# Decoding 64-bit weights on the chip: two scaled ScalarE copies and two VectorE passes in place of five VectorE passes, given out one step after the load

## The chip, the core and the metric

The kernel runs on one core of one Trainium2 chip. The core has five engines with a queue each: TensorE (PE in the profile; its weight loads are PEld), VectorE (DVE), ScalarE (ACT), GpSimd (POOL) and SyncE (SP), which here issues every DMA. An engine takes its own instructions in the order in which the program gives them out; between engines it is semaphores that order the work. The metric is the device time of one execution in microseconds, the median of the runs shown; lower is better.

## The reference

Three stages follow one another: an attention with decay over 2 batches of 8 heads, 768 tokens and 64 channels, and then two gated layers over the resulting 1536 x 512 activations.

```python
# per block of 64 tokens, with Dmask[i, j] = lam ** (i - j) for i >= j, else 0
out   = (q @ k.T * Dmask) @ v + (q * lam ** (pos + 1)) @ kv_state
kv_state = lam ** 64 * kv_state + (k * lam ** (63 - pos)).T @ v
# then, x being 1536 x 512
h = x @ w_in;   x = (h * tanh(softplus(h))) @ w_out      # layer 1, mish
h = x @ w_in2;  x = (h * sigmoid(h)) @ w_out2            # layer 2, silu
```

The four weight matrices are 512 x 2048 or 2048 x 512 and arrive as 64-bit floating-point numbers; q, k, v and lam are 32-bit.

## The kernel before

**Tiles.** The tokens are 12 chunks of 128 for the attention (n = 0 to 11, six to a batch) and three blocks of 512 for the layers (t = 0, 1, 2). The inner dimension of a layer, 2048, is cut into 16 tiles of 128; counted through both layers they are n = 0 to 31. A weight half (n, i) is one of them: (n, 0) is the 128 x 512 tile of w_in, (n, 1) that of w_out. There are 64 halves. Each is decoded once, to 32 bits, and then split in two: `wh` is the value rounded to TensorE's 32-bit matmul type by ScalarE, `wl` is what is left, by a subtraction on GpSimd (`run_parts`, L173). The activations are split in the same way (`xh`, `xl`; `gh`, `gl`), and every product is three matmuls: high by high, low by high, high by low.

**How a half comes in.** `load_w` (L71) takes one of four `slot` buffers and has SyncE issue its DMA of 512 KB. A 64-bit number lies in the slot as a low and a high 32-bit word next to each other, so a pass over the high words reads every second word. `split_w` (L86) registers a half; `begin` gives it one of four `dec` buffers; five VectorE passes (`split_op`, L122) decode it: L130 clears the sign of the high word, L132 clamps it from below, L134 shifts and masks, L136 puts in three bits of the low word, L138 puts back the sign. For the last 25 halves L94 does the first of them on ScalarE (`Abs`). After the fifth pass the slot goes back to the list, which lets `pump` (L610) load the next half. For ten pairs of tiles four more VectorE subtractions (`sum_pair`, L145, L164) make sums `t` of weights, which are split into `th`, `tl`.

**What sets the order.** The order of every engine is that in which this code calls it; nothing reorders. The code goes by steps. In each, `run_split(k)` gives out the next k VectorE passes of the list `todo`, `run_parts` the splits of the halves that are decoded, and then the step's matmuls are called. The k of each step are hand-written numbers (L634, L665, L681, L728 to L732). A VectorE or ScalarE instruction therefore stands behind all that was called before it on its engine, whether it needs that or not.

**The stages.** In the first four steps (L620) only attention chunks are worked on; x arrives in 1 MB loads that share SyncE's queue with the weights. In steps i = 0 to 7 (L643) a chunk of attention, a `w_in` product of layer 1 (`emit_h`, PE L418, then `wa` by ScalarE L399, `gh` L402, `gl` by GpSimd L403) and a `w_out` product (`emit_o`, PE L443) alternate. Within a chunk: `emit_S` (PE L305) makes scores, VectorE masks them into `sm` (L307), `emit_kd` and `emit_qd` scale k and q (ScalarE L289, GpSimd L282 and L294), GpSimd decays the state (L313), PE L326 makes `pc`, VectorE adds it to the state (L336), PE L344 and L350 make `px`, and ScalarE copies `px` to `xf` and `xh` (L358, L359). `emit_S` of the next chunk takes the two buffers that `pc` and `px` leave, so from the seventh chunk on it waits for L358.

Then come eight groups g of four tiles, less the first, which the steps above did. In the groups that begin a layer all products are plain. In the others a pair of tiles is a `Block` (L536), a fast 2 x 2 scheme whose seven products m1 to m7 (PE L557, six matmuls each) stand in the order m1, m5, m2, m6, m7, m3, m4. After m1 ScalarE copies bank `a` to bank `b` (L576), and m2 goes on accumulating in `a`, so m2 waits for that copy. In a group's second block, B, m1, m5 and m2 follow one another with nothing between; in its first block, A, a `w_out` product stands between m5 and m2. Just ahead of B, the last product of t = 2 of the group before ends and VectorE adds it to `acc` (L467, `evac`).

## Time and profile before

| | |
|---|---|
| time, median of 3 runs | 588.62 us (588.27 to 588.92) |
| span of the profiled execution | 584.0 us |
| TensorE busy | 565.3 us, 97% of the span |
| VectorE busy | 409.0 us, 70% |
| GpSimd busy | 317.1 us, 54% |
| ScalarE busy | 235.6 us, 40% |
| mean granted TensorE clock | 0.997 of full speed |

The span runs from the first to the last instruction of the profiled execution. That execution's own time is the span and what lies around it (start and end of the program), and the page gives the span alone; the median of the runs is 4.6 us above it. In a row of the timeline the columns are the start in us from the span's start, the duration in us, the engine, the line, the operation, what it writes and reads, how many instructions are merged in the row, and in brackets the idle time ahead of it with what ended that.

### The profile page before, as it was taken

What the parts mean: (1) busy time and instruction counts of PE and PEld (TensorE: products, weight loads), DVE (VectorE), ACT (ScalarE), POOL (GpSimd) and SP (SyncE); (2) the same over time, 40 slices, a digit from 0 to 9 for tenths busy, and PEclk for the clock granted to TensorE, in tenths of its full rate; (3) what the DMA queues carried; (4) which work ended last, traced back from release to release, by engine and by line L of the source; (5) the groups of instructions that cost most, each with busy time, mean ns of one, the idle gap of its engine ahead of it and who ended that gap; (6) DMA issues with size and microseconds to landing.
All of it is one profiled execution on the core that took longest, in us unless ns stands there. A gap on an engine that the chain in (4) does not pass through costs nothing.

```text
span 584.0 us, 7516 instructions
## 1 busy us (share of the span) xinstructions
PE 565.3 (97%) x2882; PEld 461.5 (79%) x2882; DVE 409.0 (70%) x509; ACT 235.6 (40%) x431; POOL 317.1 (54%) x233
## 2 busy tenths in 40 slices
PE   7689989999999999999999999999999999999997
PEld 5577768888878888888888877887888888888885
DVE  3897872769999687857798898649743993486112
ACT  2434343255424333334345465457333643344120
POOL 1767675335556364726578476737633764454320
PEclk8999999999999999999999999999999999999999
DMA  7954730003312222212312122312201140200103
GB/s 255 424 204 145 288 101 10 1 0 109 108 38 78 68 72 73 74 37 70 110 40 68 36 72 75 105 38 82 99 28 59 59 143 2 72 1 1 73 8 136
DMA packets 14627, 50.55 MB, mean 87 GB/s; under 512 B 1528, under 2 KB 3072, under 8 KB 13312
## 3 DMA queue, kind: packets, MB, share of 16 engines
q1 hardware_dynamic: 14592, 50.08, 25.1%
q8 instruction: 22, 0.36, 0.2%
q14 instruction: 13, 0.11, 0.1%
HBM read 46.92 MB, written 3.15 MB: 86 GB/s over the span
## 4 chain that ended last, share of the span: by engine, by line
PE 80%; DVE 12%; ACT 2%; DMA 2%; issue 1%; POOL 1%; SPq 0%; ACTq 0%; POOLq 0%
PE po L443 40%; PE ph L418 21%; PE b L557 7%; PE a L557 4%; PE c L557 2%; DVE dec L136 2%; PE e L557 2%; DVE dec L138 2%; DVE dec L134 1%; PE s L305 1%; DVE dec L132 1%; DVE sm L307 1%; DMA lamrow<-scr 1%; PE px L344 1%; PE px L350 1%
## 5 line engine op out<-in xcount | busy, mean ns | idle before, releaser
L403 POOL TENSOR_TENSOR gl<-wa,gh 128x512 fp32r<-128x512 f32 x96 | 144.0, 1505 | 115.1 <-PE b L557 40.4
L179 POOL TENSOR_TENSOR wl<-dec,wh 128x512 fp32r<-128x512 f32 x64 | 88.9, 1389 | 95.9 <-ACT wh L178 93.9
L467 DVE TENSOR_TENSOR acc<-po,acc 128x512 f32<-128x512 f32 x72 | 46.4, 686 | 67.0 <-PE po L443 66.9
L399 ACT ACTIVATE wa<-ph 128x512 f32<-128x512 f32 x56 | 33.6, 599 | 139.0 <-PE ph L418 135.1
L418 PE MATMUL ph<-xh,wh 128*128 128x512 f32 x224 | 87.5, 391 | 0.2 <-ACT xh L359 0.2
L418 PE MATMUL ph<-xl,wh 128*128 128x512 f32 x224 | 85.7, 389 | 0.0
L443 PE MATMUL po<-gh,wh 128*128 128x512 f32 x192 | 75.9, 395 | 0.0
L443 PE MATMUL po<-gh,wl 128*128 128x512 f32 x192 | 74.9, 390 | 0.8 <-POOL wl L179 0.8
L443 PE MATMUL po<-wh,gh 128*128 128x512 f32 x192 | 74.8, 390 | 0.5 <-ACT acc L465 0.5
L443 PE MATMUL po<-wl,gh 128*128 128x512 f32 x192 | 74.9, 390 | 0.3 <-POOL wl L179 0.3
L443 PE MATMUL po<-wh,gl 128*128 128x512 f32 x192 | 74.7, 389 | 0.0
L132 DVE TENSOR_SCALAR dec<-dec 128x512 f32<-128x512 f32 x64 | 45.4, 709 | 34.2 <-ACT dec L94 33.1
L138 DVE SCALAR_TENSOR_TENSOR dec<-slot,dec 128x512 uint32<-128x512 uint32 x64 | 67.9, 1061 | 1.9
L136 DVE SCALAR_TENSOR_TENSOR dec<-slot,dec 128x512 uint32<-128x512 uint32 x64 | 63.6, 994 | 2.1
L178 ACT CAST wh<-dec 128x512 fp32r<-128x512 f32 x64 | 39.6, 619 | 60.1 <-DVE dec L138 60.1
L418 PE MATMUL ph<-xh,wl 128*128 128x512 f32 x224 | 61.4, 389 | 0.0
L402 ACT CAST gh<-wa 128x512 fp32r<-128x512 f32 x96 | 58.7, 623 | 1.1
L134 DVE TENSOR_SCALAR dec<-dec 128x512 uint32<-128x512 uint32 x64 | 51.3, 802 | 2.0
L443 PE MATMUL po<-gl,wh 128*128 128x512 f32 x192 | 52.0, 393 | 0.0
L418 PEld LDWEIGHTS ph<-xh,wh 128*128 128x128 f32 x224 | 42.0, 188 | 9.4 <-ACT xh L359 0.4
L418 PEld LDWEIGHTS ph<-xh,wl 128*128 128x128 f32 x224 | 42.0, 188 | 8.8
L418 PEld LDWEIGHTS ph<-xl,wh 128*128 128x128 f32 x224 | 42.0, 188 | 8.8
(107 smaller groups left out, 874.7 us busy)
## 6 DMA issues: line engine op xcount, KB each, us to landing
slot<-w SPq DMA_DIRECT2D x64, 512.0 KB, 3.7
xslot<-x SPq DMA_DIRECT2D x10, 1024.0 KB, 9.4
out<-acc SPq DMA_DIRECT2D x12, 256.0 KB, 2.0
xslot<-x SPq DMA_DIRECT2D x4, 512.0 KB, 4.3
dmask<-scr SPq DMA_DIRECT2D x2, 256.0 KB, 4.0
lamrow<-scr SPq DMA_DIRECT2D x2, 128.0 KB, 6.0
pw<-lam SPq DMA_DIRECT2D x1, 0.0 KB
scr<-pw SPq DMA_DIRECT2D x1, 8.0 KB
```

Source lines behind the costliest of these rows:

```text
L132: nc.vector.tensor_scalar(out=df, in0=df, scalar1=2.0**-15, scalar2=None, op0=ALU.max)
L134: nc.vector.tensor_scalar(out=d, in0=d, scalar1=3, scalar2=0x3FFFFFF8, op0=shl, op1=band)
L136: nc.vector.scalar_tensor_tensor(out=d, in0=low, scalar=29, in1=d, op0=shr, op1=bor)
L138: nc.vector.scalar_tensor_tensor(out=d, in0=high, scalar=0xC0000000, in1=d, op0=band, op1=bor)
L178: nc.scalar.copy(hi, f)
L179: nc.gpsimd.tensor_tensor(out=lo, in0=f, in1=hi.bitcast(F32), op=ALU.subtract)
L402: nc.scalar.copy(gh, a)
L403: nc.gpsimd.tensor_tensor(out=gl, in0=a, in1=gh.bitcast(F32), op=ALU.subtract)
L418: nc.tensor.matmul(ph, lhsT=wi[wsel][:, kk * P : (kk + 1) * P], rhs=xt[xsel][:, kk, :], start=(i == 0), stop=(i == 3 * KD - 1),)
L443: nc.tensor.matmul(po[t][j], lhsT=lhsT, rhs=rhs, start=(first and wsel + gsel == 0), stop=(last and gsel == 1))
L467: nc.vector.tensor_tensor(out=acc[:, j, :], in0=po[t][j], in1=acc[:, j, :], op=ALU.add)
L557: nc.tensor.matmul(self.b[dst], lhsT=w[ws][:, kk * P : (kk + 1) * P], rhs=x[xx][:, kk, :], start=(start and i == 0), stop=(i == 5), skip_g ...
```

## The change

The five passes become four, on two engines. ScalarE copies the high words, read as 32-bit floats and scaled by 2^-112, to `dec`; it then copies the low words, read as integers, in place in the slot, scaled and shifted so that the three bits remain that L136 took by a shift. VectorE shifts `dec` left by three and puts in the three bits (new L126), and puts back the sign (new L130). All 64 halves go this way; the `Abs` copies are gone.

The order changes too. A counter `tick` goes up at the end of each step. `begin`, which now holds the two ScalarE copies, runs for a half at the earliest in a later step than its load was issued in (`age`), and the VectorE passes at the earliest in a later step than `begin`. The hand-written k are gone: `run_split(2)` is called in nearly all steps, `run_split(1)` in a `Block`'s, and `run_pre` starts one half, or two in an attention step. In the attention the halves are registered all ten at once, so that they no longer wait for the step that named them. In the groups `run_parts` is called ahead of the step's matmuls for all that is decoded. The matmuls stand in the same order as before.

```diff
     def load_w(n, i):
+        loaded[n, i] = tick[0]
@@
-            if on_act:
-                nc.scalar.activation(decs[n, i].bitcast(F32), raws[n, i][:, :, 1].bitcast(F32), AF.Abs)
+            begun[n, i] = tick[0]
+            low, high = raws[n, i][:, :, 0], raws[n, i][:, :, 1]
+            nc.scalar.activation(decs[n, i].bitcast(F32), high.bitcast(F32), AF.Copy, scale=2.0**-112)
+            nc.scalar.activation(low, low, AF.Copy, scale=TOP3, bias=2.0**-21 - 0.5)
@@
-            if k == 4:
+            if k == 1:
                 slots.append(held.pop((n, i)))
                 parts.append((*wtiles[n, i], decs[n, i].bitcast(F32), (n, i)))
@@
-    def run_pre(now=False):
-        while pre and (now or (len(uses) < WD and pre[0][0] in raws)):
-            assert len(uses) < WD
+    def run_pre(k=1, age=1):
+        while k and pre and len(uses) < WD and pre[0][0] in raws and tick[0] - loaded[pre[0][0]] >= age:
             pre.pop(0)[1]()
-            now = False
+            k -= 1
@@
         if k == 0:
-            nc.vector.tensor_scalar(out=d, in0=high, scalar1=0x7FFFFFFF, scalar2=None, op0=band)
-        elif k == 1:
-            nc.vector.tensor_scalar(out=df, in0=df, scalar1=2.0**-15, scalar2=None, op0=ALU.max)
-        elif k == 2:
-            nc.vector.tensor_scalar(out=d, in0=d, scalar1=3, scalar2=0x3FFFFFF8, op0=shl, op1=band)
-        elif k == 3:
-            nc.vector.scalar_tensor_tensor(out=d, in0=low, scalar=29, in1=d, op0=shr, op1=bor)
+            nc.vector.scalar_tensor_tensor(
+                out=d, in0=d, scalar=3, in1=low, op0=ALU.logical_shift_left, op1=ALU.bitwise_or
+            )
         else:
-            nc.vector.scalar_tensor_tensor(out=d, in0=high, scalar=0xC0000000, in1=d, op0=band, op1=bor)
+            nc.vector.scalar_tensor_tensor(
+                out=d, in0=high, scalar=0x80000000, in1=d, op0=ALU.bitwise_and, op1=ALU.bitwise_or
+            )
@@
     def run_split(k):
-        for _ in range(min(k, len(todo))):
-            todo.pop(0)()
-        run_pre()
+        while k and todo and (todo[0][0] is None or begun.get(todo[0][0], tick[0]) < tick[0]):
+            todo.pop(0)[1]()
+            k -= 1
@@ attention, first four steps
         if n == 1:
-            split_w(0, 0)
-        if n == PH - 2:
-            split_w(1, 0)
-            split_w(0, 1)
-        run_split((0, 3, 5, 3)[n])
+            for half in ((0, 0), (1, 0), (0, 1), (2, 0), (1, 1), (3, 0), (2, 1), (3, 1), (4, 0), (5, 0)):
+                split_w(*half)
+        run_split(2)
         finish = emit_O(n)
+        run_pre(1 + (n == PH - 1))
@@ steps i
-        run_split((6, 3, 4, 4, 4, 4, 4, 4, 4, 0, 0, 0)[i])
+        run_split(2)
...
             xfinish = emit_O(n)
+        run_pre(2)
...
-        run_split((2, 0, 4, 4, 4, 4, 4, 4, 0, 0, 0, 5)[i])
+        run_split(2)
         pump()
+        tick[0] += 1
@@ groups
             run_later()
-            k = len(parts)
+            run_parts()
+            if item[0] is idle or item[0] in fills or item[0] in os:
+                run_pre()
             for fn in item:
                 fn()
-            run_parts(k)
...
-            run_split(k)
+            run_split(1 if isinstance(getattr(item[0], "__self__", None), Block) else 2)
             pump()
+            tick[0] += 1
```

VectorE in the third step of the attention, from the state of chunk 1 to the mask of chunk 3; `sm<-s` are the masks, two to a chunk, and slot_84 holds the first half. Before:

```order
L336 TENSOR_TENSOR state_101<-pc,state_101 64x4x64 x2
L130 TENSOR_SCALAR dec<-slot_84 128x512
L132 TENSOR_SCALAR dec<-dec 128x512
L134 TENSOR_SCALAR dec<-dec 128x512
L307 TENSOR_TENSOR sm<-s_265,dmask 128x512
L307 TENSOR_TENSOR sm<-s_266,dmask 128x512
```

After:

```order
L330 TENSOR_TENSOR state_101<-pc,state_101 64x4x64 x2
L301 TENSOR_TENSOR sm<-s_264,dmask 128x512
L301 TENSOR_TENSOR sm<-s_265,dmask 128x512
L356 TENSOR_TENSOR xl<-xf,xh 128x4x128
L330 TENSOR_TENSOR state_102<-pc,state_102 64x4x64 x2
L126 SCALAR_TENSOR_TENSOR dec<-dec,slot_84 128x512
L130 SCALAR_TENSOR_TENSOR dec<-slot_84,dec 128x512
```

The three passes that stood between the state of chunk 1 and the mask of chunk 2 are gone, and the two that are left stand behind that mask.

ScalarE in step i = 1, from the `xh` of chunk 5 to the `xf` of chunk 6. Before:

```order
L359 CAST xh<-xf 128x4x128
L402 CAST gh<-wa 128x512
L399 ACTIVATE wa<-ph 128x512
L178 CAST wh_480<-dec 128x512
L289 ACTIVATE kd<-xslot_109,dmask 128x64 x4
L358 COPY xf<-px 128x512
```

After:

```order
L353 CAST xh<-xf 128x4x128
L98 ACTIVATE dec<-slot_86 128x512
L99 ACTIVATE slot_86<-slot_86 128x512
L98 ACTIVATE dec<-slot_87 128x512
L99 ACTIVATE slot_87<-slot_87 128x512
L396 CAST gh<-wa 128x512
L172 CAST wh_460<-dec 128x512
L393 ACTIVATE wa<-ph 128x512
L172 CAST wh_533<-dec 128x512
L283 ACTIVATE kd<-xslot_109,dmask 128x64 x4
L352 COPY xf<-px 128x512
```

Four copies and one more rounding to `wh` now stand between two `xf` copies.

ScalarE at the start of block B of the third group (g = 2): the copy of bank `a` to bank `b`, and what stands ahead of it. `th` is the upper half of a sum of weights. Before:

```order
L399 ACTIVATE wa<-b 128x512
L402 CAST gh<-wa 128x512
L178 CAST wh_1811<-dec 128x512
L576 COPY b<-a 128x512
L581 COPY m_1924<-e 128x512
```

After:

```order
L393 ACTIVATE wa<-b 128x512
L396 CAST gh<-wa 128x512
L98 ACTIVATE dec<-slot_86 128x512
L99 ACTIVATE slot_86<-slot_86 128x512
L172 CAST th<-t_1826 128x512
L570 COPY b<-a 128x512
L172 CAST wh_1807<-dec 128x512
L575 COPY m_1891<-e 128x512
```

VectorE at the same place, after the change:

```order
L158 TENSOR_TENSOR t_1826<-dec 128x256
L158 TENSOR_TENSOR t_1826<-dec,t_1826 128x256
L158 TENSOR_TENSOR t_1826<-dec 128x256
L461 TENSOR_TENSOR acc<-po,acc 128x512 x4
L158 TENSOR_TENSOR t_1826<-dec,t_1826 128x256
L126 SCALAR_TENSOR_TENSOR dec<-dec,slot_85 128x512
L130 SCALAR_TENSOR_TENSOR dec<-slot_85,dec 128x512
```

The `th` that now stands ahead of the copy needs the fourth subtraction, and that now stands behind the four additions to `acc`; before, the subtractions of this pair were all ahead of them.

## Rows read from the trace of the kernel before

**Rows 1.** Engines' busy time, share of the span and instructions, from the page.

```profile
PE 565.3 (97%) x2882; PEld 461.5 (79%) x2882; DVE 409.0 (70%) x509; ACT 235.6 (40%) x431; POOL 317.1 (54%) x233
```

**Rows 2.** Busy time by stretch: length, then PE, PEld, DVE, ACT, POOL, clock, DMA.

```profile
17.87:99.19 81.32, 72.34 (x643) 57.02 (x642) 64.08 (x90) 34.10 (x76) 56.22 (x47) 1.00 0.52 193
99.19:340.00 240.81, 240.81 (x1077) 198.72 (x1076) 194.25 (x223) 96.15 (x163) 132.41 (x90) 1.00 0.19 61
340.00:410.00 70.00, 68.72 (x300) 55.62 (x299) 54.35 (x56) 38.68 (x70) 47.06 (x32) 1.00 0.24 76
410.00:578.35 168.35, 168.35 (x744) 139.41 (x743) 86.74 (x121) 60.94 (x108) 76.04 (x56) 1.00 0.15 51
```

**Rows 3.** Timeline of PE, 17 to 100 us: where it waits, and three scores.

```profile
21.75 0.43 PE L350 MATMUL px<-sm,xslot 128*64 128x128 f32 x2 [1.01 <-DVE sm L307]
...
28.64 0.43 PE L350 MATMUL px<-sm,xslot 128*64 128x128 f32 x2 [2.42 <-DVE sm L307]
...
42.78 1.16 PE L344 MATMUL px<-qd,state 128*128 128x128 f32 x8 [1.34 <-POOL qd L294]
...
53.23 1.16 PE L305 MATMUL s<-xslot 64*128 64x128 f32 x14 [0.29 <-ACT xf L358]
...
64.51 1.16 PE L305 MATMUL s<-xslot 64*128 64x128 f32 x16 [0.25 <-issue]
...
74.25 1.52 PE L305 MATMUL s<-xslot 64*128 64x128 f32 x16
...
87.14 1.16 PE L305 MATMUL s<-xslot 64*128 64x128 f32 x14 [0.81 <-ACT xf L358]
...
96.91 1.16 PE L305 MATMUL s<-xslot 64*128 64x128 f32 x16
```

**Rows 4.** Timeline of DVE ahead of the first wait of rows 3.

```profile
18.15 1.17 DVE L130 TENSOR_SCALAR dec<-slot 128x512 uint32<-128x512 uint32 x1
```

**Rows 5.** Timelines of ACT and POOL in the attention.

```profile
21.96 1.07 ACT L289 ACTIVATE kd<-xslot,dmask 128x64 f32<-128x64 f32 x4 [2.74 <-DMA xslot<-x]
...
85.03 0.62 ACT L178 CAST wh<-dec 128x512 fp32r<-128x512 f32 x1 [2.64 <-DVE dec L138]
...
26.31 1.27 POOL L179 TENSOR_TENSOR wl<-dec,wh 128x512 fp32r<-128x512 f32 x1 [2.01 <-ACT wh L178]
```

**Rows 6.** Groups by line: count, busy us and mean ns, idle before.

```profile
L134 DVE TENSOR_SCALAR dec<-dec 128x512 uint32<-128x512 uint32 x64 | 51.3, 802 | 2.0
...
L132 DVE TENSOR_SCALAR dec<-dec 128x512 f32<-128x512 f32 x64 | 45.4, 709 | 34.2 <-ACT dec L94 33.1
...
L130 DVE TENSOR_SCALAR dec<-slot 128x512 uint32<-128x512 uint32 x39 | 30.6, 785 | 0.0
...
L94 ACT ACTIVATE dec<-slot 128x512 f32<-128x512 f32 x25 | 16.0, 671 | 1.1 <-DMA slot<-w 0.8 <-POOL wl L179 0.3
...
L358 ACT COPY xf<-px 128x512 f32<-128x512 f32 x12 | 6.9, 576 | 7.3 <-PE px L350 7.3
...
L450 ACT CAST sh<-tmp 128x1024 fp32r<-128x1024 f32 x2 | 2.1, 1062 | 0.0
```

**Rows 7.** Timelines of DVE, PE and ACT at the start of block B, group 2.

```profile
208.69 2.48 DVE L467 TENSOR_TENSOR acc<-po,acc 128x512 f32<-128x512 f32 x4 [2.13 <-PE po L443]
...
210.53 0.62 PE L557 MATMUL e<-sh,th 128*128 128x512 f32 x2
...
210.72 0.57 ACT L576 COPY b<-a 128x512 f32<-128x512 f32 x1 [1.21 <-PE a L557]
...
211.88 0.62 PE L557 MATMUL a<-xh,wh 128*128 128x512 f32 x2
```

**Rows 8.** Timeline of DVE: the shortest and the longest weight subtraction here.

```profile
199.42 0.42 DVE L164 TENSOR_TENSOR t<-dec,t 128x256 f32<-128x256 f32 x1
...
364.66 1.52 DVE L164 TENSOR_TENSOR t<-dec 128x256 f32<-128x256 f32 x1
```

**Rows 9.** DMA issues of weight halves: count, KB each, us to landing, from the page.

```profile
slot<-w SPq DMA_DIRECT2D x64, 512.0 KB, 3.7
```

More of the change, by code (lines that the diff above doesn't have):

```diff
@@ L74, in load_w @@
         raws[n, i] = held[n, i].bitcast(U32).rearrange("p (c two) -> p c two", two=2)
+    TOP3 = 2.0**-29 * (1 - 2.0**-20)
+    tick = [0]
+    loaded, begun = {}, {}
     ready = set()
@@ L106, in split_w @@
         pre.append(((n, i), begin))
-        todo.extend(lambda k=k: op(k) for k in range(int(on_act), 5))
-    def run_pre(now=False):
-        while pre and (now or (len(uses) < WD and pre[0][0] in raws)):
-            assert len(uses) < WD
+        todo.extend(((n, i), lambda k=k: op(k)) for k in range(2))
+    def run_pre(k=1, age=1):
+        while k and pre and len(uses) < WD and pre[0][0] in raws and tick[0] - loaded[pre[0][0]] >= age:
             pre.pop(0)[1]()
-            now = False
+            k -= 1
     def used(key):
@@ L169, in op @@
                 used((b, 0))
-        todo.extend(lambda k=k: op(k) for k in range(4))
+        todo.extend((None, lambda k=k: op(k)) for k in range(4))
     def run_parts(k=None):
@@ L629, in decay_attention_mish_silu_kernel @@
         if n == 1:
-            split_w(0, 0)
-        if n == PH - 2:
-            split_w(1, 0)
-            split_w(0, 1)
-        run_split((0, 3, 5, 3)[n])
+            for half in ((0, 0), (1, 0), (0, 1), (2, 0), (1, 1), (3, 0), (2, 1), (3, 1), (4, 0), (5, 0)):
+                split_w(*half)
+        run_split(2)
         finish = emit_O(n)
+        run_pre(1 + (n == PH - 1))
         run_parts()
         pump()
+        tick[0] += 1
     later.append(finish)
-    halves = {0: [(2, 0)], 1: [(3, 0), (1, 1)], 3: [(2, 1), (3, 1), (4, 0), (5, 0)]}
     for i, (t, f) in enumerate(steps):
@@ L652, in decay_attention_mish_silu_kernel @@
             split_pair(3)
-        for half in halves.get(i, ()):
-            split_w(*half)
         if n < N:
@@ L717, in decay_attention_mish_silu_kernel @@
         for at, item in enumerate(items):
-            if g == NG and at == 7:
-                silu.append(True)
             run_later()
-            k = len(parts)
+            run_parts()
+            if item[0] is idle or item[0] in fills or item[0] in os:
+                run_pre()
             for fn in item:
                 fn()
-            run_parts(k)
             run_rest(1)
             run_sums(1)
-            small = isinstance(getattr(item[0], "__self__", None), Block)
-            k = 1 if small else 0 if item[0] is idle else 3 if item[0] in hs or at < (8 if first else 11) else 2
-            if g == NG and at < 8:
-                k = (1, 1, 1, 2, 2, 2, 2, 2)[at]
-            elif g == NG - 1 and at == len(items) - 1:
-                k = 0
-            run_split(k)
+            run_split(1 if isinstance(getattr(item[0], "__self__", None), Block) else 2)
             pump()
+            tick[0] += 1
         fills = [lambda n=n0 + f: emit_o(2, n, n % GF == 0, n % GF == GF - 1) for f in range(GF)]
```

6 lines of the change are left out of this document (removed).

## The prediction

> **What bounds the kernel now.** I read the engines' busy time first, then busy time by stretch, then the timeline of TensorE where it has gaps, and last the queue of whoever ends each gap. TensorE is busy for 565.3 of 584.0 us [rows 1], so 18.7 us is all that an edit can take out that leaves the matmuls alone, as this one does. By stretch [rows 2], TensorE is busy without a gap from 99.19 to 340 and from 410 to 578.35; it is idle for 81.32 - 72.34 = 8.98 us between 17.87 and 99.19 and for 1.28 us between 340 and 410. The remaining 8.4 us lie ahead of 17.87, where the first loads and the decay table are waited for, and behind 578.35, where the last sums are stored; the change touches neither. So VectorE's 409 us, though large, cost nothing in most of the span: they matter where TensorE has gaps. There the timeline [rows 3] names the causes: twice the mask `sm` of VectorE (1.01 and 2.42 us), once `qd` of GpSimd (1.34), and ScalarE's `xf` (0.29; and 0.81 at 87.14, where the two matmuls ahead had already waited). A gap costs more than its idle time, since the first matmuls behind it take longer. I therefore measure by distances between scores. From 64.51 to 74.25 is a step without a wait, 9.74 us. From 53.23 to 96.91 there are four steps, 43.68 us, which is 43.68 - 4 x 9.74 = 4.7 us more than four such steps.
>
> **What is removed.** L130 39 times at 785 ns, L132 64 times at 709 and L134 64 times at 802 [rows 6]: 30.6 + 45.4 + 51.3 = 127.3 us of VectorE. The two passes that are left keep their operands, two SBUF inputs each, and I cost them as before. From 99.19 to 340 and behind 410 the removal is worth nothing, since TensorE had no gap there to give back; all that it can do is harm.
>
> **What is added.** 128 ScalarE copies less the 25 of L94, 103 in all. The trace has the first kind: L94 reads every second word of a slot, 671 ns [rows 6]. It does not have the second kind, which also writes every second word and converts integers. Its bounds are a plain copy of 512 elements, 576 ns (L358), and one of 1024, 1062 ns (L450, as if each skipped word counted) [rows 6]. I take 671, the row with the same reading, and keep 1062 for the range. A gain below 576 is excluded, since no row of 512 elements on ScalarE is shorter. That is 103 x 0.671 = 69 us, and ScalarE goes from 235.6 to about 305 us, 53% of the span. Most of it lies beside matmuls. The DMAs keep their order on SyncE but for two slots that change places; a slot comes free after its second VectorE pass. The copies now stand in ScalarE's queue behind a load, so a late load would hold `xf`, `gh` and all behind it. A half lands 3.7 us after its issue [rows 9], and `age` keeps its copies a step away, 9.7 us here, so I cost this at nothing; in the first steps, where x fills the queue, up to 1 us.
>
> A rule of the Trainium skill speaks against the trade: ScalarE: Activation LUTs, section Rules for kernel authors, wants additions and multiplications on VectorE and not on ScalarE. In the trace a copy (671 ns) is no dearer than a pass that it replaces (709 to 802), so the rows do not bear it out for this pair; by the rule ScalarE would become the dearer place, which is the first rival. The same page's 186 ns + 0.833 ns per element makes an estimate of 0.61 us for 512 elements, beside the 0.67 of the row.
>
> **The attention, up to the score at 53.23.** The mask of chunk 2 stood behind three passes, of which the first ran from 18.15 for 1.17 us [rows 4]. Now nothing stands between, and the first wait is gone. The next score then wants chunk 3 at about 21.7, but its load lands only when `kd` starts, at 21.96 [rows 5]: 0.3 us of a new wait. The mask of chunk 3 stands behind two passes in place of five and comes at about 25.3 in place of 28.6. Then the gain shrinks. GpSimd's first `wl` waited for ScalarE's `wh` until 26.31 [rows 5], and its decay of the state, `kd` and `qd` stand behind it. That `wh` now stands behind two copies for the next half, so it is no earlier, and neither is GpSimd. VectorE waits for that decay ahead of the next passes, and so the mask of chunk 4 comes at about 33 and `qd` of chunk 5 at 39.6 (before, 42.78). Behind that ScalarE is late: between two `xf` it now has four copies (2.68 us), five casts or activations at 0.62 (the size of the `wh` in rows 5), `kd` 1.07 and `xf` itself 0.58, 7.4 us in all. That is less than a step of 9.74, so it is no bound in the long run, but it comes to it late. I reach 50.4 to 51.3 for the score that was at 53.23. **Term one: 2.35 us less, from 1.9 to 2.8.** With 1062 ns for the second copy, six of which lie on this way, 6 x 0.39 = 2.3 us of it go back.
>
> **The attention, from there to 96.91.** Of the 4.7 us, the larger part is at 87.14: ScalarE's `wh` waited for the last VectorE pass until 85.03 [rows 5], with `kd` and `xf` queued behind it, and TensorE waited for that `xf`. In the new order the ten halves of the attention are decoded two to a step, and the last pass of the last stands two steps ahead of there. What is late next is GpSimd, which has two `wl` in a row ahead of `kd`, `xl`, the decay and `qd`: by its busy share, 56.22 of 81.32 us [rows 2], it fits, with up to 1 us lost. **Term two: 4.3 us less, from 3.7 to 4.7.**
>
> **340 to 410.** The gaps there end on `acc` copies, on a `wl` and on the bank copy of a block, all queued behind late passes; ScalarE's three `Abs` copies in a row ahead of that bank copy are spread out now. **Term three: 1.3 us less, from 0.8 to 1.3.**
>
> **A new wait at the start of block B.** The second product m2 waits for the copy of bank `a` to `b`. In group 2 `a` is ready when that copy starts, at 210.72, and m2 starts at 211.88 without a wait [rows 7]. Now a `th` stands ahead of that copy on ScalarE, and it needs the fourth subtraction, which stands behind the four additions to `acc` on VectorE. These end at 208.69 + 2.48 = 211.17 [rows 7]. The subtraction takes 0.42 to 1.52 us [rows 8], `th` 0.62, the copy 0.57: 212.8 to 213.9, so m2 is 0.9 to 2.0 us late. I take 1.0, near the short one, since GpSimd has little to do there. Group 3 repeats group 2. In groups 6 and 7 the product that precedes goes bank by bank, the additions start earlier, and the same chain ends about when m2 is due: 0 to 1 us, taken as 0.2. Block B of group 5 has no additions on VectorE ahead of it. **Term four: 2.4 us more, from 0.9 to 4.**
>
> The long and the short subtraction differ by whether GpSimd is reading at the same time. The Trainium skill, SBUF — State Buffer, section SBUF: two separate sides, says that a VectorE instruction with two SBUF inputs and a GpSimd instruction exclude each other for the whole of one; if that fell on all four subtractions, the block cost would be 2.0 us each in groups 2 and 3 and 1.0 in 6 and 7, and the sum 3.6 us worse. No row shows which will overlap.
>
> **The sum.** -2.35 - 4.3 - 1.3 + 2.4 = -5.55 us, from 584.0 to 578.5 us of span. The span of before stands 4.6 us under the median of its runs; I take that distance as unchanged, so the time is 588.6 - 5.5 = 583.1 us.
>
> **Rivals.**
> - ScalarE becomes the bound in the first steps: the second copy takes 1062 ns. Against it stands that L94's stride costs under 0.1 us; for it, that no row shows a strided write. Term one is then 0 and term two 4.0: -4.0 - 1.3 + 2.4 = -2.9, 585.7 us. Chance 0.20.
> - The loads hold the early chunks: the first wait becomes one for x. For it, the `kd` at 21.96 that waited 2.74 us for a load [rows 5]; against it, a DMA share of 0.52 over the stretch [rows 2]. Term one is 0: -4.3 - 1.3 + 2.4 = -3.2, 585.4 us. Chance 0.12.
> - No change: GpSimd's two `wl` in a row keep `qd` late in every step, and term two is 0: -2.35 - 1.3 + 2.4 = -1.2, 587.4 us. For it, that GpSimd ends a gap already (42.78); against it, that in four steps 9.74 us each leave room. Chance 0.10.
> - Slower: ScalarE's queue at the start of block B. Behind the copy of `a` a further `wh` waits for two passes, then the copy `m`, then the addition that m7 needs. If VectorE's passes meet GpSimd there, m2 loses 2.0 us and m7 another 1, 3 us in each of four blocks: -7.95 + 12 = +4, 592.7 us. It decides from (7.95 + 1.2) / 4 = 2.3 us a block. Against it, that m7 comes two products and an output product after the copy. Chance 0.08.
>
> My forecast has 0.50. About 0.2% (1.2 us) is what a measurement of this kernel can tell from no change. Faster: 0.50 + 0.20 + 0.12 = 0.82; same 0.10; slower 0.08. The best case is -2.8 - 4.7 - 1.3 + 0.9 = -7.9, 580.7, and a little less if the matmuls behind the closed gaps shorten too; at the other end the range takes in the rivals down to the one of no change: 580 to 587.5.
>
> **What would show it.** Right, if VectorE's busy time falls to about 282 us and ScalarE's rises to about 305, with the second copy near 0.67 us; if the waits for `sm` at 21.75 and 28.64 are gone, while a wait for `qd` and one for `xf` in steps 0 to 2 remain; if four steps to the last score take close to 39 us; and if m2 of block B waits about 1 us for the bank copy in groups 2 and 3. Wrong, if TensorE waits between 99 and 578 us anywhere else, above all for a `wl` or `th` of a half that is given out later than before, or if the gaps of the attention are still about 9 us in sum with new names.

## The result, and the profile of the changed kernel

| | before | after |
|---|---|---|
| time, us (median; lowest to highest) | 588.46 (588.27 to 588.92) | 583.4 (582.84 to 583.96) |
| ratio, 95% interval | | 0.9916, 0.9902 to 0.993 |
| span of the profiled execution, us | 584.0 | 581.9 |
| time of that execution, us | not given | 583.96 |

The change makes the kernel 0.84% faster; 583.1 us had been predicted, with a range of 580 to 587.5. The time came out within 0.3 us. The way to it did not: the span was predicted to fall to 578.5 us, and the page shows 581.9. Two errors of about 3 us, one in the span and one in what lies between span and time, cancelled, so that the time came out this close is in part luck. Both are taken apart below.

The engines' busy time of the changed kernel (as [rows 1]) and the groups of the four instructions that now make up a half's conversion (as [rows 6]; L98 and L99 are the scaled copies, L126 and L130 the two passes):

```profile
PE 567.1 (97%) x2882; PEld 462.5 (79%) x2882; DVE 282.4 (49%) x342; ACT 294.4 (51%) x534; POOL 312.5 (54%) x233
```

```profile
L98 ACT ACTIVATE dec<-slot 128x512 f32<-128x512 f32 x64 | 42.6, 665 | 0.4 <-DMA slot<-w 0.4
L99 ACT ACTIVATE slot<-slot 128x512 uint32<-128x512 uint32 x64 | 42.4, 663 | 0.0
...
L126 DVE SCALAR_TENSOR_TENSOR dec<-dec,slot 128x512 uint32<-128x512 uint32 x64 | 71.1, 1110 | 92.6 <-ACT slot L99 64.5 <-issue 26.5 <-POOL kd L276 1.5
L130 DVE SCALAR_TENSOR_TENSOR dec<-slot,dec 128x512 uint32<-128x512 uint32 x64 | 64.3, 1004 | 2.2
```

VectorE is at 282.4 us as predicted, and the second copy, whose price no row of before showed, takes 663 ns, as much as the first. The rival in which it takes 1062 falls with that row. ScalarE was expected at 305 us and is at 294.4: copies that follow one another overlap by 0.1 us (46.74 to 47.42, the next from 47.32), so that 664 ns for each counts too much. The two passes that are left mean 1110 and 1004 ns, where they meant 994 and 1061 before.

The timeline of TensorE in the changed kernel, where it waits (the last bracket: idle us, and who ended it), and some of the scores (L299, as [rows 3]):

```profile
18.44 1.16 PE L299 MATMUL s<-xslot 64*128 64x128 f32 x16
...
25.29 0.43 PE L344 MATMUL px<-sm,xslot 128*64 128x128 f32 x2 [0.16 <-DVE sm L301]
...
26.90 1.16 PE L299 MATMUL s<-xslot 64*128 64x128 f32 x16
...
31.84 1.20 PE L412 MATMUL ph<-xl,wh 128*128 128x512 f32 x4 [1.44 <-DVE xl L356]
...
35.70 1.16 PE L299 MATMUL s<-xslot 64*128 64x128 f32 x16
...
40.68 1.16 PE L338 MATMUL px<-qd,state 128*128 128x128 f32 x8 [0.86 <-POOL qd L288]
...
52.66 1.52 PE L299 MATMUL s<-xslot 64*128 64x128 f32 x14 [1.67 <-ACT xf L352]
...
63.98 1.16 PE L299 MATMUL s<-xslot 64*128 64x128 f32 x16
...
93.20 1.16 PE L299 MATMUL s<-xslot 64*128 64x128 f32 x16
```

Two scores of the kernel before, the third and the fifth, in the same view:

```profile
17.87 1.16 PE L305 MATMUL s<-xslot 64*128 64x128 f32 x16
...
30.26 1.16 PE L305 MATMUL s<-xslot 64*128 64x128 f32 x16
```

The two waits for the mask `sm` (1.01 and 2.42 us in [rows 3]) are gone but for 0.16 us. Scores are counted here from the first chunk on; the one at 18.44 is the third, the one at 93.20 the last. From the score at 18.44 to the one at 26.90 it is 8.46 us, where it was 30.26 - 17.87 = 12.39. But of these 3.9 us the next three steps give back 2.8, from 26.90 to 52.66 in 25.76 us where it was 53.23 - 30.26 = 22.97: there are new waits for `xl` and for `xf`. From 63.98 on the three steps to the last score at 93.20 take 9.74 us each.

### The profile page after: what moved, and what is told of

The parts are those of the page before. It is cut to its first block, busy times and chain, and to the rows that moved or that the text cites. A ratio compares the mean times of both kernels' runs of the same rounds, so it can differ in the third digit from the quotient of the medians.

```text
span 581.9 us, 7445 instructions
## 1 busy us (share of the span) xinstructions
PE 567.1 (97%) x2882; PEld 462.5 (79%) x2882; DVE 282.4 (49%) x342; ACT 294.4 (51%) x534; POOL 312.5 (54%) x233
## 4 chain that ended last, share of the span: by engine, by line
PE 85%; DVE 4%; ACT 4%; DMA 4%; issue 2%; SPq 0%; POOL 0%; ACTq 0%; DVEq 0%; POOLq 0%
PE po L437 43%; PE ph L412 25%; PE b L551 7%; PE a L551 4%; PE c L551 2%; DVE acc L461 2%; DMA slot<-w 2%; PE e L551 1%; PE px L338 1%; DMA lamrow<-scr 1%; PE px L344 1%; PE s L299 1%; DVE dec L126 1%; ACT th L172 1%; ACT slot L99 1%
## 5 line engine op out<-in xcount | busy, mean ns | idle before, releaser
L397 POOL TENSOR_TENSOR gl<-wa,gh 128x512 fp32r<-128x512 f32 x96 | 136.6, 1427 | 195.3 <-ACT gh L396 116.6
L126 DVE SCALAR_TENSOR_TENSOR dec<-dec,slot 128x512 uint32<-128x512 uint32 x64 | 71.1, 1110 | 92.6 <-ACT slot L99 64.5
L173 POOL TENSOR_TENSOR wl<-dec,wh 128x512 fp32r<-128x512 f32 x64 | 91.0, 1423 | 25.5 <-ACT wh L172 18.9
L130 DVE SCALAR_TENSOR_TENSOR dec<-slot,dec 128x512 uint32<-128x512 uint32 x64 | 64.3, 1004 | 2.2
L437 PEld LDWEIGHTS po<-wh,gh 128*128 128x128 f32 x192 | 36.0, 188 | 9.0 <-ACT acc L459 1.5
L98 ACT ACTIVATE dec<-slot 128x512 f32<-128x512 f32 x64 | 42.6, 665 | 0.4 <-DMA slot<-w 0.4
```

The costliest lines, as they stand in the source:

```text
L98: nc.scalar.activation(decs[n, i].bitcast(F32), high.bitcast(F32), AF.Copy, scale=2.0**-112)
L126: nc.vector.scalar_tensor_tensor(out=d, in0=d, scalar=3, in1=low, op0=ALU.logical_shift_left, op1=ALU.bitwise_or)
L130: nc.vector.scalar_tensor_tensor(out=d, in0=high, scalar=0x80000000, in1=d, op0=ALU.bitwise_and, op1=ALU.bitwise_or)
L173: nc.gpsimd.tensor_tensor(out=lo, in0=f, in1=hi.bitcast(F32), op=ALU.subtract)
L397: nc.gpsimd.tensor_tensor(out=gl, in0=a, in1=gh.bitcast(F32), op=ALU.subtract)
L437: nc.tensor.matmul(po[t][j], lhsT=lhsT, rhs=rhs, start=(first and wsel + gsel == 0), stop=(last and gsel == 1))
```

## The experiments

Times are medians; a ratio is to the kernel before, run beside it (its medians there: 587.4 to 588.2 us). An edit is shown against the changed kernel unless it says otherwise.

**What the page of before stands for.** The kernel before, unchanged.

> The kernel before, unchanged, run several times with the span of each run. The prediction took 4.6 us as the distance between span (584.0) and time (588.6); the runs of the changed kernel show 2.1 us between the two. Theory A: the page's span is of one execution that was shorter than the timed ones, and the distance is 2.1 us for both kernels: then the spans of these runs lie near 586.4 and the times near 588.5, and the span has fallen by 5 us as the time has. Theory B: what lies around the span differs between the kernels: then the spans here stay near 584.0, the distance near 4.5, and 2.5 us of the gain have come from outside the traced span.

Its runs, and those of the same kernel beside the other experiments, had spans from 584.1 to 588.8 us, median 585.8, and the time lay 1.7 to 1.9 us above the span in each. For the changed kernel it is 2.1. So neither theory holds as it was put. Theory B falls: 4.6 us never lay around the span. Theory A has the cause right, with 1.8 us in place of 2.1: the page of before showed an execution at the fast end, some 1.8 us under the middle. What differs between its executions can be seen by stretch (length; PE, PEld, DVE, ACT, POOL; granted clock; DMA), here around a gap that both traces have, at 85.87 to 87.14 in the kernel before ([rows 3] have its end) and 1 us later in this one:

```profile
86.00:88.00 2.00, 0.46 (x2) 0.29 (x2) 0.78 (x3) 1.94 (x6) 1.24 (x2) 1.00 0.38 131
88.00:90.00 2.00, 1.83 (x15) 1.61 (x16) 0.75 (x2) 0.73 (x2) 1.76 (x3) 0.72 0.44 131
90.00:92.00 2.00, 2.00 (x6) 1.52 (x6) 0.54 (x1) 1.61 (x4) 2.00 (x3) 0.50 0.00 0
92.00:94.00 2.00, 2.00 (x10) 1.61 (x9) 0.00 (x0) 0.95 (x2) 1.33 (x2) 0.93 0.00 0
```

Behind the gap the granted clock falls to 0.50 (1.2 GHz), and the step from this score to the next takes 11.29 us (88.17 to 99.46) where it took 9.77 in [rows 3]. The page of before had full clock there (1.00 in [rows 2]).

The two traces differ at the start too. In this one the clock is at 0.50 from 16 to 20 us, and the third and the eighth score are these:

```profile
20.63 1.16 PE L305 MATMUL s<-xslot 64*128 64x128 f32 x16
...
54.00 1.39 PE L305 MATMUL s<-xslot 64*128 64x128 f32 x16
```

The third comes 2.8 us later than on the page of before, and the first of the two waits for `sm` is not there.

**The arithmetic without the order.** Against the kernel before: its own order, places and counts, and only the operations replaced.

```
-            if on_act:
-                nc.scalar.activation(decs..., raws[n, i][:, :, 1]..., AF.Abs)
+            nc.scalar.activation(decs..., high..., AF.Copy, scale=2.0**-112)
+            nc.scalar.activation(low, low, AF.Copy, scale=TOP3, bias=2.0**-21 - 0.5)
...
-        if k == 0: ... elif k == 1: ... elif k == 2: ... elif k == 3: ... else: ...
+        if k == 3: (shift, or)  elif k == 4: (and, or)
```

> The two scaled ScalarE copies and two VectorE passes in the old order: the copies are given out where the old order began a half, the two passes where the fourth and fifth pass stood, nothing where the first three stood. Theory (the gain needs the new order): in the old order the copies go out in the same step as the passes that want them, so that VectorE waits for ScalarE with masks and additions queued behind it; the waits for the mask near 21.75 and 28.64 get new names, and the time is 586 to 590. Rival (fewer VectorE passes are the whole gain): 582 to 584.5, as the changed kernel or better, and better by up to 1.6 us if the order at the start of block B, which is the old one here, is worth that: no wait of m2 near 208 and 272.

587.86 us, ratio 1.0001 (0.9988 to 1.0015): nothing is gained, although VectorE falls to 277.3 us. The theory's time holds, but not the wait that it named: TensorE waits for no mask of VectorE. It is ScalarE that is late. From its trace, ScalarE and TensorE at the three places that cost most:

```profile
26.25 0.66 ACT L95 ACTIVATE dec<-slot 128x512 f32<-128x512 f32 x1 [2.48 <-DMA slot<-w]
```

```profile
28.07 2.05 PE L342 MATMUL px<-qd,state 128*128 128x128 f32 x8 [4.68 <-ACT xf L356]
...
67.56 1.66 PE L303 MATMUL s<-xslot 64*128 64x128 f32 x14 [3.42 <-ACT xf L356]
...
407.34 0.73 PE L555 MATMUL a<-xh,wh 128*128 128x512 f32 x2 [2.08 <-ACT b L574]
```

A copy that is given out in the step of its load waits 2.48 us for that load, and `xf` stands behind it: TensorE waits 4.68 us. At 67.56 and 407.34 three halves are begun in a row, six copies of 0.66 to 0.70 us ahead of `xf` and of the bank copy (at 67.56 a fourth half follows, which waits for its load again). The same three halves stand ahead of the bank copy in groups 2 and 3 too, and m2 waits 0.63 us in each, where the rival had expected no wait. This is what the change's step between load and copies is for, and it is the danger that the prediction named in the paragraph on what is added.

**The order without the arithmetic.** The old five passes, three where the changed kernel has its first and two where it has its second; no scaled copies.

> The old five VectorE passes, no ScalarE copies, in the new order: three passes where the new order has its first, two where it has its second. Theory (the order needs the shorter arithmetic): VectorE has some 400 us of work again, ten halves of about 4.2 us = 42 us of it in the first seven steps of the attention, two halves to a step of 9.74 us beside masks and additions; it falls behind there, and the time is 588 to 593. Rival (giving the halves out earlier is the gain, whatever the arithmetic): 583 to 585.

631.55 us, ratio 1.0747 (1.072 to 1.0774). The theory's direction holds and its size does not: most of the 44 us are lost behind the attention, in which the third score to the last take 87.88 us (20.53 to 108.41) where 79.04 were on the page of before. In block B of five groups the product m7 waits 2.2 to 2.5 us for VectorE, and ahead of block A of group 5 an output product waits longer:

```profile
235.61 1.22 PE L553 MATMUL b<-sh,th 128*128 128x512 f32 x2 [2.17 <-DVE c L561]
...
393.52 0.79 PE L439 MATMUL po<-wh,gh 128*128 128x512 f32 x1 [5.92 <-ACT acc L461]
```

The addition `c` stands behind ten passes in a row there (226.41 to 234.95 us for the first of these waits), and `acc` behind a `wh` that waits for VectorE. So the order lives from a half costing VectorE two passes, and the two parts of the change, each put in by itself as here, are worth nothing, or less.

**The casts behind the products.** In the dense layers the casts `wh`, `th` and their subtractions go behind an item's products and copies again, as in the kernel before.

```
             run_later()
-            run_parts()
+            k = len(parts)
             ...
             for fn in item:
                 fn()
+            run_parts(k)
```

> The changed kernel, but in the dense layers' part the casts wh and th with their subtractions on GpSimd stand behind an item's products and copies again, as in the kernel before. Theory: the waits of m2 for the bank copy near 208.45 and 271.99 (0.64 us of idle time, 0.81 us of delay each) vanish, and so does the wait for the acc copy near 359.07 (1.07 us of idle time): 1.6 + 1.1 = 2.7 us less, a time near 580.7, a ratio to before of 0.987. Rival: the delay moves on, since wh and wl come a copy later, and TensorE waits for a wl, th or gl somewhere between 100 and 576 instead: 583 to 584.

579.05 us, ratio 0.9854 (0.9834 to 0.9875), more gain than expected: from the last score to the end it is 4.4 us shorter than in the changed kernel, of which 2.7 are at the starts of block B and 1.6 between those of groups 3 and 5. TensorE has no wait of 0.2 us or more left from 59 us to the last product. The stretch of [rows 2] that held the gaps of term three, in this kernel:

```profile
340.00:405.00 65.00, 65.00 (x288) 53.61 (x287) 27.29 (x28) 37.32 (x68) 39.77 (x29) 1.00 0.21 67
```

The start of block B in group 2, first in the changed kernel (PE, then ACT), then here (PE, ACT); [rows 7] are the same place before:

```profile
206.29 0.62 PE L551 MATMUL e<-sh,th 128*128 128x512 f32 x2
...
208.45 0.74 PE L551 MATMUL a<-xh,wh 128*128 128x512 f32 x2 [0.64 <-ACT b L570]
...
209.96 0.63 PE L551 MATMUL b<-sh,th 128*128 128x512 f32 x2
...
207.29 0.62 ACT L172 CAST th<-t 128x512 fp32r<-128x512 f32 x1 [2.37 <-DVE t L158]
207.82 0.58 ACT L570 COPY b<-a 128x512 f32<-128x512 f32 x1
```

```profile
205.50 0.62 PE L551 MATMUL e<-sh,th 128*128 128x512 f32 x2
...
206.85 0.62 PE L551 MATMUL a<-xh,wh 128*128 128x512 f32 x2
...
208.22 0.62 PE L551 MATMUL b<-sh,th 128*128 128x512 f32 x2
...
205.69 0.57 ACT L570 COPY b<-a 128x512 f32<-128x512 f32 x1 [1.25 <-PE a L551]
206.50 0.62 ACT L172 CAST th<-t 128x512 fp32r<-128x512 f32 x1 [0.24 <-DVE t L158]
```

From `e` to the `b` product it is 3.67 us in the changed kernel and 2.72 here. With `th` ahead of it the bank copy started at 207.82; behind it, as soon as bank `a` was ready. So the cost of term four comes from the place of the casts.

**The wait for `xl`.** In the fourth step the passes of half (1, 0) are moved ahead of the state's additions.

```
+        if n == PH - 1:
+            run_split(2)
         emit_state(n)
         ...
-        run_split(2)
+        if n < PH - 1:
+            run_split(2)
```

> The changed kernel, but in the fourth step of the attention the two passes of half (1, 0) stand on VectorE ahead of the additions to the state, which wait for GpSimd's decay, and no longer between these and the subtraction xl of chunk 3. Theory (xl waited for these passes, a wait that the prediction left out): the wait for xl at 31.84 (1.44 us of idle time) vanishes, the score that stood at 35.70 comes 1.4 us earlier, and if nothing later takes it up, the time is 1.4 us less, 582.0. Rival: the wait for qd of GpSimd at 40.68 or for xf at 52.66 grows by as much, since GpSimd and ScalarE set the pace of these steps: 583.4 and the score at 52.66 unmoved.

583.29 us, ratio 0.9917: no change. The rival holds. The wait for `xl` is still 1.15 us, since the two passes now run beside GpSimd's decay (1.53 and 1.00 us) and push the additions and `xl` back; and the wait for `qd` grew from 0.86 to 1.19.

**Fewer copies on ScalarE.** One half begun in a step of the attention in place of two (`run_pre(2)` to `run_pre(1)`).

> The changed kernel, but each step of the attention from the fifth on begins one half, not two: two scaled copies on ScalarE between two xf in place of four, until all ten halves are begun. Theory (ScalarE's queue is what makes xf late at 52.66): the wait of 1.67 us there vanishes, the steps behind keep 9.74 us, and the time is 1.7 us less, 581.7, and up to 1 us less still if the clock no longer falls to 0.50 behind the gap. Rival (wh waits for VectorE's passes, which run 1.6 to 1.8 us each beside GpSimd, and that alone holds kd and xf): the wait stays at 1 us or more and the time at 583. A third outcome: halves begun later arrive late, and TensorE waits for a wl or wh between 60 and 110 us.

583.51 us, ratio 0.9921: no change, and the score behind the wait stands at 52.63, where it stood. The rival holds: the copies are not what makes `xf` late. In its trace `wh` waits for VectorE until 44.14, as in the changed kernel:

```profile
44.14 0.62 ACT L172 CAST wh<-dec 128x512 fp32r<-128x512 f32 x1 [3.48 <-DVE dec L130]
```

**The casts behind `xf`.** The second group of casts in a step of the attention goes behind `kd`, `xf` and `xh`.

```
-            run_parts()
+            if i == 0:
+                run_parts()
             emit_state(n)
             ...
             xfinish = emit_O(n)
+            run_parts()
```

> The changed kernel, but in the attention's steps the second group of casts wh, with their wl on GpSimd, stands behind kd, xf and xh of the step and not ahead of them. Theory (as in the run with two copies): the wh that waits 3.24 us for VectorE until 44.11 no longer holds kd and xf; the wait for xf at 52.66 falls by about 1 us, 582.4, if wl, which comes later, is not waited for. Rival (the four copies alone hold xf): the wait stays near 1.67 and the time at 583.4.

582.49 us, ratio 0.9904 (0.9884 to 0.9923). The expected 582.4, but the interval holds the changed kernel's 0.9916 too, so the time alone does not decide. In the trace the wait ahead of that score is 1.12 us in place of 1.67, and it is no longer one for `xf`, which ends at 49.70. It ends with the other buffer that the score needs, `pc`, which VectorE copies behind two passes of 1.80 and 1.67 us:

```profile
51.06 0.85 DVE L328 COPY state<-pc 64x256 f32<-64x256 f32 x2
...
52.01 1.16 PE L299 MATMUL s<-xslot 64*128 64x128 f32 x16 [1.12 <-issue]
```

The step that ends there takes 9.53 us in place of 9.87, and the one ahead of it, with a wait for `qd` of 1.06 us in place of 0.86, takes 7.28 in place of 7.09. So the casts did hold `xf`, and what that gave back is mostly taken up again.

**Three edits at once**: the first, second and third of the last four.

> Three edits of the changed kernel together: casts behind an item's products and copies in the dense layers, the passes of half (1, 0) ahead of the additions to the state, and one half begun in a step of the attention in place of two. Theory (the three waits are independent): 579.05 of the first alone, less 1.4 for xl and 1.7 for xf, is 575.9, a ratio to before of 0.980. Rival (the waits of the attention hand one gain to the next): 577.5 to 579, with a wait for qd or xf grown.

580.26 us, ratio 0.9863 (0.9841 to 0.9885): no better than the casts alone. The rival holds in its direction (it said 577.5 to 579); what `xl` and `xf` were thought to give is handed on, as in the runs of each.

**`wl` on VectorE.** In the attention the ten subtractions `wl` go from GpSimd to VectorE, behind the passes of their step.

```
-            nc.gpsimd.tensor_tensor(out=lo, in0=f, in1=hi.bitcast(F32), op=ALU.subtract)
+            (nc.gpsimd if late else nc.vector).tensor_tensor(out=lo, ...)
```

> The changed kernel, but the ten subtractions wl of the attention run on VectorE, behind the passes of their step, and not on GpSimd. Theory (VectorE's passes and GpSimd's subtractions lengthen each other, and that sets the pace from 28 to 53 us: the eight passes from 33.8 to 44 took 1.4 to 1.8 us each where the undisturbed ones take 0.69): GpSimd loses 10 x 1.27 us, VectorE gains 10 x 0.68; the passes there fall towards 0.7 to 1.1, and the waits for xl at 31.84, qd at 40.68 and xf at 52.66 (1.44 + 0.86 + 1.67 = 4.0 us) fall below 1.5 together, so that the time is 580.9 or less. Rival (the order of the queues sets the pace, not the lengthening): a wl on VectorE waits for its cast with masks and state additions behind it, new waits take the place of the old, 583 or more.

582.13 us, ratio 0.9906 (0.9889 to 0.9923): between the theory's 580.9 and the rival's 583, and not told apart from the changed kernel's 0.9916. VectorE in the changed kernel (first), and at the same place here:

```profile
36.01 1.76 DVE L126 SCALAR_TENSOR_TENSOR dec<-dec,slot 128x512 uint32<-128x512 uint32 x1
37.81 1.68 DVE L130 SCALAR_TENSOR_TENSOR dec<-slot,dec 128x512 uint32<-128x512 uint32 x1
```

```profile
36.31 0.69 DVE L126 SCALAR_TENSOR_TENSOR dec<-dec,slot 128x512 uint32<-128x512 uint32 x1
37.04 0.69 DVE L130 SCALAR_TENSOR_TENSOR dec<-slot,dec 128x512 uint32<-128x512 uint32 x1
37.65 0.68 DVE L181 TENSOR_TENSOR wl<-dec,wh 128x512 fp32r<-128x512 f32 x1
```

Two passes and a subtraction take 2.0 us here, where the two passes took 3.5 beside GpSimd's `xl` and `qd`. The waits for `qd` (0.53) and ahead of the score at 51.31 (0.74) are shorter, but the one for `xl` stays (1.42). From the third score to the last it is 73.28 us (18.28 to 91.56) where the changed kernel took 74.76; but there the clock fell, as is shown below, and the kernel with the casts behind, whose attention is the same and whose clock held, took 73.81 (18.60 to 92.41). So the lengthening is a cause, and this edit is worth about 0.5 us of these steps, trace against trace. It does not end the lengthening: of the five passes that took over 1.4 us from 33.79 to 44.08 in the changed kernel, two still take 1.74 and 1.64 here (39.57 and 41.34), beside GpSimd's `qd` and `gl`. And the passes still stand ahead of `xl`.

**Both moves of the casts**, in the dense layers and in the attention.

> The changed kernel with both edits of the casts: behind an item's products and copies in the dense layers (579.05 alone), and behind kd, xf and xh in the attention (582.49 alone, beside 583.4). If the two are independent: 579.05 - 0.9 = 578.1. If not, 579.

578.57 us, ratio 0.9862 (0.9836 to 0.9887): not told apart from the dense layers' move alone. The wait for `qd` is 1.72 us here.

**`wl` on VectorE, and the casts behind the products.**

> The changed kernel with wl on VectorE in the attention and the casts behind an item's products and copies in the dense layers. If the lengthening sets the pace in the attention, 579.05 - 2.5 = 576.5, below both the kernel before and the changed one; if not, 579 or more.

577.37 us (576.55 to 578.64), ratio 0.9833 (0.9813 to 0.9853): 1.7% below the kernel before, and below the changed kernel's interval. This is the best median of the versions here, but its interval overlaps that of the casts' move alone (0.9834 to 0.9875). From the third score to the last it takes 72.93 us.

**And `xl` ahead of the passes**, in that version: the passes of half (1, 0) behind `xl` and the mask.

```
-        run_split(2)
+        if n < PH - 1:
+            run_split(2)
         ...
-        run_split(2)
+        run_split(2 if i else 4)
         run_lows()
```

> The kernel of the run with wl on VectorE and the casts behind (577.37), and in it the two passes of half (1, 0) moved from ahead of xl of chunk 3 to behind the mask that follows it. Theory (these two passes alone make xl late): the wait for xl, 1.43 us in that kernel, falls below 0.3 and the score behind it comes 1.2 us earlier; with the step behind it paced by the matmuls, the time is 576.2. Rival (the wait is handed on, as when the passes were put ahead of the state additions): the wait for qd (0.48) or for xf (0.76) grows by as much, and the time stays within 0.5 us of 577.4, or half (1, 0), two steps later now, comes late for its matmuls.

579.33 us, ratio 0.9864 (0.9845 to 0.9882). The wait for `xl` is gone, and from the score at 19.54 to the one at 35.62 it takes 16.08 us, 1.5 less than in the version above. So these two passes alone held `xl`. But each half comes a little later from there on, and the rival's last case came about, a wait for the `wl` of a late half:

```profile
58.05 1.20 PE L424 MATMUL ph<-xh,wl 128*128 128x512 f32 x4 [2.82 <-DVE wl L181]
```

From the third score to the last it takes 73.64 us, 0.7 more than the version above. The rest of the difference between the two traces (577.4 and 574.5 us of span) is mostly the third score, at 19.54 in place of 17.27, ahead of which the edit changes nothing: the time of this run tells less than its waits.

## Why the prediction was right, and where it was not

| term | predicted | page against page |
|---|---|---|
| one: up to the score at 53.23 | -2.35 | -1.14 |
| two: from there to the last score | -4.3 | -3.14 |
| three: 340 to 410 | -1.3 | -0.65 |
| four: m2 of block B | +2.4 | +2.68 |
| start of the run | 0 | +0.57 |
| not placed | | -0.4 |
| span | -5.55 | -2.1 |

The first two come from distances between scores: 35.36 to 34.22 us and 43.68 to 40.54. The third is the way from `e` of group 3 to the `b` product of group 5, 133.00 us before and 133.30 after, less the 0.95 of term four within it.

Of what is not placed, 0.5 us is one output product, 3.24 us long in the kernel before (169.20 to 172.44) and 2.72 in the changed one, as its neighbours are in both: the prediction's "worth nothing" for 99.19 to 340 was wrong by that.

**Term one** is half of what was predicted. The waits for `sm` went as described. The step that failed is "VectorE waits for that decay ahead of the next passes", which was followed to the mask of chunk 4 alone: the `xl` of chunk 3 stands in the same queue, behind the same passes, and TensorE waits for it first. The passes are also costed "as before", at their means, when from 29 to 44 us of the changed kernel six of them take 1.4 to 1.8 us beside GpSimd. For what is late next, the prediction counted ScalarE's copies; the run with two copies in place of four shows that they were not it, and the runs with the casts behind `xf` and with `wl` on VectorE that the lengthened passes were part of it.

Both terms are measured against a single execution of the kernel before. In its second trace the third score to the eighth takes 33.4 us, less than the 34.22 of the changed kernel, and the eighth to the last 45.5, more than the 43.68 of [rows 3]. Against that trace term one gives nothing and term two 4.9 us. How the gain divides between start, term one and term two depends on the executions that are compared; up to the last score it is 3.7 us against the one and 6.3 against the other.

**Term two** has its mechanism right: the three steps behind 63.98 take 9.74 us each, and four such would take the 39 that was forecast, where the four took 40.54. The shortfall is a single step, 52.66 to 63.98, of 11.32 us. By stretch, the granted clock in the changed kernel there, and in the kernel with the casts behind, whose wait for `xf` is as long (1.64 us) and whose step takes 10.03 us:

```profile
52.00:54.00 2.00, 1.34 (x14) 1.22 (x14) 0.20 (x1) 1.97 (x5) 2.00 (x3) 0.82 1.01 426
54.00:56.00 2.00, 2.00 (x6) 1.51 (x6) 1.97 (x4) 2.00 (x4) 2.00 (x3) 0.50 0.60 254
56.00:58.00 2.00, 2.00 (x9) 1.63 (x8) 2.00 (x2) 0.68 (x2) 2.00 (x2) 0.82 0.00 0
```

```profile
54.00:56.00 2.00, 2.00 (x10) 1.60 (x9) 2.00 (x3) 2.00 (x5) 2.00 (x3) 1.00 0.77 324
```

So 1.3 us of term two were lost to the clock in this execution, and without that the term is about -4.4.

**Term three** was mis-sized, since the gap at 361.69 was expected to close. It is 1.07 us now. ScalarE's `acc` copies stand behind a `wh` that waits for VectorE:

```profile
357.92 0.62 ACT L172 CAST wh<-dec 128x512 fp32r<-128x512 f32 x1 [3.20 <-DVE dec L130]
358.44 2.04 ACT L459 COPY acc<-po 128x512 f32<-128x512 f32 x4
```

It is the same move of the casts ahead of an item's copies that makes term four. The prediction looked for it at the start of block B and not here. With the casts behind, both are gone.

**Term four** was right in its mechanism and nearly in its size: 0.95 us each in groups 2 and 3 (predicted 1.0), 0.39 each in groups 6 and 7 (0.2). m7 never waited, so the slower rival did not come about; nor did the one of late loads or the one of ScalarE as the bound, in this order. In the old order a late load of a weight half and six copies in a row held TensorE, for 4.68 and 3.42 us, though the second copy was no dearer there (0.63 to 0.70 us).

**The distance between span and time** is the step that hid all this. "I take that distance as unchanged" took 4.6 us that the kernel before does not have. Its page shows an execution whose span, 584.0, is 1.8 us under the median of 585.8; the time is 1.8 us above the span, and 2.1 for the changed kernel. Counted from the median span, the changed kernel's spans (580.7 to 581.9) are some 4.5 us shorter; the times that were taken side by side differ by 5.1, and against the second trace of the kernel before (586.6) the span falls by 4.7. That what this has beyond the 2.1 us of the two pages is fewer falls of the clock would fit the stretches above and the mean granted clocks (median 0.991 over the 66 runs of the kernel before, 0.991 to 0.997 in the four of the changed one, 0.997 on the page of before), but no run here shows its size.

## What to carry to other kernels

Fewer instructions on an engine that is not the bound, paid for on another, gave nothing in the old order; the new order without them cost 44 us; and in the new order one moved list of casts lost some 3.6 us (the ratios 0.9916 and 0.9854, of 588) of what the two together could have won. When a list is moved ahead of an item, go through each queue that it enters and name everything that now stands behind its longest wait, at every kind of item and not at the one where it was looked for. Before adding terms to the span of a page, find out from repeated executions where in their range that page lies.

## What the hardware showed that was not expected

**What is shared by VectorE and GpSimd.** Each of the three removed passes took 0.41 to 0.43 us when GpSimd did not run and up to 1.5 beside it; the two that are left take 0.69 and up to 1.79. The means of [rows 6] hide that the change took away the cheap ones, and the prediction's "no dearer than a pass that it replaces" holds for the means alone: by itself a pass was shorter than the 0.67 of a copy. One of them in the trace of before, first by itself, then while GpSimd's `gl` runs from 360.11 to 362.10:

```profile
353.95 0.43 DVE L134 TENSOR_SCALAR dec<-dec 128x512 uint32<-128x512 uint32 x1
...
360.88 1.49 DVE L134 TENSOR_SCALAR dec<-dec 128x512 uint32<-128x512 uint32 x1
```

GpSimd's instructions are lengthened as well, from 1.27 to 1.75 us. Beside the two passes of the changed kernel at 36.01 and 37.81 (shown with the run of `wl` on VectorE) it ran these:

```profile
35.94 1.29 POOL L173 TENSOR_TENSOR wl<-dec,wh 128x512 fp32r<-128x512 f32 x1 [1.27 <-ACT wh L172]
37.19 1.75 POOL L356 TENSOR_TENSOR xl<-xf,xh 128x512 fp32r<-128x512 f32 x1
38.90 1.73 POOL L288 TENSOR_TENSOR qd<-xslot,lamrow 128x512 f32<-128x512 f32 x1
```

The five end in turn: `wl` at 37.23, a pass at 37.77, `xl` at 38.94, a pass at 39.49, `qd` at 40.63. Each pass ends 0.5 us behind the GpSimd instruction ahead of it, and `xl` and `qd` 1.1 to 1.2 us behind a pass, so the two engines worked one after the other. The Trainium skill, SBUF — State Buffer, section SBUF: two separate sides, describes this as a lock on a shared pair of ports, held for a whole instruction. The ends in the trace agree with that; the prediction weighed the rule for four subtractions in block B and not for the passes of the attention, where it mattered.

**A copy in place over every second word** of a slot, integers in and out, costs ScalarE 663 ns for 512 elements, as much as one that only reads so (665). No row of before showed such a write, and the prediction gave 1062 ns for it a chance of 0.20.

**The clock behind a gap.** The fall to 0.50 behind TensorE's gap near 52 us is not certain. With 1.6 us or more of gap there (the changed kernel, and the runs with the casts behind, with `xl` first, with two copies, and with three edits; in the last two it is two gaps of 0.9 and 0.8 with two matmuls between) the step behind it took 11.3 us in four of the five traces and 10.03 in the other. With gaps of 1.12 us or less (the casts behind `xf`, both moves of the casts, and the two with `wl` on VectorE in which `xl` was left) the clock stayed at 1.00. Longer gaps elsewhere were not always followed by a fall: the one near 87 us of the kernel before (1.4 and 0.8 us) was in one of its two traces, the 2.82 us at 58.05 in the last run was not. The start is as uncertain: in four of the fourteen traces the clock was at 0.50 from 16 to 18 us, and the third score came at 19.5 to 20.6 us; in the other ten it was at 1.00, and the score came at 17.3 to 18.6. So a closed gap is worth more than its length in some executions, and a single trace can't say in how many.
